# Backward attention: each mask product directly behind its score pair, the dP pair behind both

## Chip, cores, metric

One core of one Trainium2 chip runs the whole kernel. The metric is the time of one execution on the device in microseconds (us). The kernel before takes 2784.18 us (median of 2 executions, 2774.3 to 2794.06). Executions of a kernel on one core are called slow when they are over 1.5% above the fastest of the same kernel, and fast otherwise.

## The reference, cut to what matters

Four residual layers, linear attention (A) and sliding-window attention (B) in turn, forward and then all gradients. The change touches only the backward pass of the two B layers:

```python
scores = einsum("bhqd,bhkd->bhqk", q, k) * (Dh ** -0.5)        # S = 2048, H = 32, Dh = 20, W = 256
mask   = (idx[:, None] - idx[None, :] >= 0) & (idx[:, None] - idx[None, :] < W)
p      = softmax(where(mask, scores, -1e9))
o      = einsum("bhqk,bhkd->bhqd", p, v)
# backward, per block of 128 queries: e = exp(scores + mask), dP = dO v^T, ds = e * dP,
# dv from e, dk and dq from ds
```

## The kernel before

A *unit* is one block of 128 queries of one group of four heads; it sees up to three blocks of 128 keys. There are 8 groups x 16 blocks = 128 units per layer. Four heads fit beside each other in the partitions, 32 rows each, so every score product and every dP product is a matmul on one 32-row tile of TensorE's 128 x 128 array. A half unit is two heads. The steps have short names in this text: **S** scores (2 matmuls of up to 384 columns, 32 rows each), **D** dP (the same shape), **M** mask (2 full-array matmuls of 256 columns that add -30000 where the mask forbids), **F** six transposes of ds (full array), **V** value and key products (16 matmuls on 32-column tiles), **Q** dq products (12 of them).

```python
psl = self.pool(st, "atl", 3)
...
ps_sp = self.pool(st, "pss", 3, PSUM)      # 3 slots: scores and dP tiles
ps_o  = self.pool(st, "pso", 2, PSUM)      # 2 slots: F, V and Q accumulators
...
def scores(u, half, ta, tb):               # S with ("QT","KT"), D with ("dOT","VT")
    ps = ps_sp.tile([P, 2, 512], F32, name="sp")
    for j in range(2):
        r0 = HP * (2 * half + j)           # row tile of the head: 0, 32, 64 or 96
        ...
            nc.tensor.matmul(ps[:, j, ...], lhsT=slabs[..][ta][r0:r0 + HP, qs],
                             rhs=slabs[..][tb][r0:r0 + HP, ...],
                             start=(a == k0), stop=(ta == "dOT"), tile_position=(r0, 0), ...)
    return ps

def mask(u, ps):                           # M
    ...
        nc.tensor.matmul(o, lhsT=self.ident, rhs=self.far, start=False, stop=True, ...)

def expo(u, half, ps):   # ScalarE:  e  = exp(c * ps)          [cut]
def dscore(u, half, ps): # VectorE:  ds = ps * e; for half 0 a DMA transposes ds   [cut]
def flip(u):             # F, for half 1; the copy out is VectorE's in even units, ScalarE's in odd ones
...
for s in range(n + LAG):                   # TensorE runs in exactly this order
    ...                                    # loads cut
    if s < n:
        sc = scores(s, 0, "QT", "KT")
    if 0 <= s - 3 < n:
        dscore(s - 3, 1, scores(s - 3, 1, "dOT", "VT"))
    if s < n:
        mask(s, sc)
        expo(s, 0, sc)
    if 0 <= s - 4 < n:
        flip(s - 4)
    if s < n:
        sc = scores(s, 1, "QT", "KT")
    if 0 <= s - 2 < n:
        dscore(s - 2, 0, scores(s - 2, 0, "dOT", "VT"))
    if s < n:
        mask(s, sc)
        expo(s, 1, sc)
    key_products(s)                        # V
    if 0 <= s - LAG < n:
        dq(s - LAG)                        # Q
```

So a unit is S D M F S D M V Q on TensorE, and the S and D that stand side by side use different halves of the rows.

The softmax here doesn't subtract the row's maximum and nothing guards it: scores larger than these inputs give would overflow.

## Time and profile before

| | before |
|---|---|
| time | 2784.18 us (2774.3 to 2794.06) |
| profiled execution | 2776.2 us, mean granted TensorE clock 0.894 |
| the two stages of the change | 985-1390 and 1720-2125 us |

The table of stretches gives the busy time of each engine in a stretch, then the granted TensorE clock (PEclk, a share of full speed), the DMA share and GB/s. The engines stand in the order PE (TensorE's matmuls), PEld (its weight loads), DVE (VectorE), ACT (ScalarE), POOL (GpSimd), each with its number of instructions behind an x. These are the two stages in the kernel before:

```profile
985.00:1390.00 405.00, 338.82 (x5744) 194.50 (x5744) 280.29 (x384) 274.16 (x448) 3.22 (x6) 0.93 0.77 156
1720.00:2125.00 405.00, 343.39 (x5744) 196.29 (x5744) 280.49 (x384) 274.48 (x448) 1.40 (x3) 0.92 0.77 153
```

TensorE 84%, VectorE 69%, ScalarE 68%: none is full. Next, the page's slices of the span, the granted clock in tenths, one digit for every 69 us. Digits 15 to 20 and 25 to 31 are the stages.

```profile
PEclk9789898778886879999889898999997998999999
```

The groups of instructions of the whole span (busy us, mean ns | idle of the engine before them, and what ended most of it):

```profile
L797 DVE TENSOR_TENSOR ds<-sp,e 128x768 bf16<-128x768 f32 (+2 forms) x512 | 464.5, 907 | 225.7 <-PE sp L758 171.8
L786 ACT ACTIVATE e<-sp 128x768 bf16<-128x768 f32 (+2 forms) x512 | 393.3, 771 | 207.6 <-PE sp L771 146.3
L758 PE MATMUL sp<-VT,dOT 32*128 32x384 bf16 (+2 forms) x1152 | 173.9, 309 | 45.4 <-DVE ds L797 42.2
L758 PE MATMUL sp<-KT,QT 32*128 32x384 bf16 (+2 forms) x1152 | 174.4, 317 | 26.7 <-DMA KT<-qkvT_139 9.7
L771 PE MATMUL sp<-far,ident 128*128 128x256 bf16 x896 | 184.8, 290 | 0.0
```

D (third line) waits for VectorE's product ds. One unit of the timeline, TensorE alone, full clock (start us, us, line, tiles, count, idle before):

```profile
1312.65 0.34 PE L758 MATMUL sp<-KT,QT 32*128 32x384 bf16 x2
1312.88 0.34 PE L758 MATMUL sp<-VT,dOT 32*128 32x384 bf16 x2
1313.15 0.39 PE L771 MATMUL sp<-far,ident 128*128 128x256 bf16 x2
1313.38 0.50 PE L808 MATMUL acc<-ident,ds 128*128 128x128 bf16 x6
1313.82 0.33 PE L758 MATMUL sp<-KT,QT 32*128 32x384 bf16 x2
1314.34 0.34 PE L758 MATMUL sp<-VT,dOT 32*128 32x384 bf16 x2 [0.19 <-DVE ds L797]
1314.61 0.39 PE L771 MATMUL sp<-far,ident 128*128 128x256 bf16 x2
1315.13 0.51 PE L830 MATMUL acc<-e,dOsl 128*32 128x256 bf16 x16
1315.46 0.35 PE L851 MATMUL acc<-dsT,ksl 128*32 128x128 bf16 x12
```

The starts are what counts, since the ends of matmuls are modelled. D to D is 1.46 us (1312.88 to 1314.34). That is one turn of a loop: in the built program every dP tile of this stretch has the same slot in PSUM (where the matmuls write), so D waits until VectorE has read the previous dP tile to form ds.

### The profile page before, as it was taken

What the parts mean: (1) busy time and instruction counts of PE and PEld (TensorE: products, weight loads), DVE (VectorE), ACT (ScalarE), POOL (GpSimd) and SP (SyncE); (2) the same over time, 40 slices, a digit from 0 to 9 for tenths busy, and PEclk for the clock granted to TensorE, in tenths of its full rate; (3) what the DMA queues carried; (4) which work ended last, traced back from release to release, by engine and by line L of the source; (5) the groups of instructions that cost most, each with busy time, mean ns of one, the idle gap of its engine ahead of it and who ended that gap; (6) DMA issues with size and microseconds to landing.
All of it is one profiled execution on the core that took longest, in us unless ns stands there. A gap on an engine that the chain in (4) does not pass through costs nothing.

```text
span 2776.2 us, 66240 instructions
## 1 busy us (share of the span) xinstructions
PE 2305.0 (83%) x27132; PEld 1398.2 (50%) x27132; DVE 1393.4 (50%) x2932; ACT 1379.6 (50%) x2467; POOL 556.5 (20%) x835
## 2 busy tenths in 40 slices
PE   6589998569997578888779696888885987899999
PEld 4345555334544334545447474454543665664654
DVE  6444554333431556777658475776774774500000
ACT  4247666326676357777534464777773445500000
POOL 1124444124455400000033231000001331100000
PEclk9789898778886879999889898999997998999999
DMA  6698886388885878788553575787785448596652
GB/s 204 207 180 172 176 172 164 98 185 180 177 166 140 202 199 161 160 167 157 103 172 127 132 197 178 158 158 159 151 149 145 147 150 197 155 240 152 208 181 66
DMA packets 827824, 457.63 MB, mean 165 GB/s; under 512 B 649088, under 2 KB 771968, under 8 KB 825472
## 3 DMA queue, kind: packets, MB, share of 16 engines
q1 hardware_dynamic: 637568, 237.34, 42.1%
q10 hardware_dynamic: 176768, 168.86, 22.0%
q0 software_dynamic: 13184, 47.20, 5.8%
q8 instruction: 212, 3.47, 0.5%
q14 instruction: 92, 0.75, 0.1%
HBM read 173.41 MB, written 148.50 MB: 116 GB/s over the span
## 4 chain that ended last, share of the span: by engine, by line
PE 53%; DVE 11%; DMA 7%; ACT 7%; issue 4%; POOL 2%; SPq 2%; ACTq 2%; DVEq 0%; POOLq 0%
PE wg L1058 12%; PE d L594 9%; DVE ds L797 6%; PE sp L758 5%; PE d L332 4%; PE acc L830 3%; PE sp L771 3%; PE s L370 3%; ACT dsT L813 3%; PE d L150 2%; PE d L229 2%; PE d L551 2%; PE d L244 2%; ACTq L133 2%; PE d L627 1%
## 5 line engine op out<-in xcount | busy, mean ns | idle before, releaser
L797 DVE TENSOR_TENSOR ds<-sp,e 128x768 bf16<-128x768 f32 (+2 forms) x512 | 464.5, 907 | 225.7 <-PE sp L758 171.8
L786 ACT ACTIVATE e<-sp 128x768 bf16<-128x768 f32 (+2 forms) x512 | 393.3, 771 | 207.6 <-PE sp L771 146.3
L372 ACT ACTIVATE e<-s 128x768 bf16<-128x768 f32 (+2 forms) x512 | 374.2, 774 | 150.2 <-PE s L370 105.1
L1058 PE MATMUL wg<-wg_r,wg_l 128*128 128x480 bf16 (+1 forms) x1920 | 349.3, 345 | 10.6 <-DMA wg_r<-in_grad_out_dram 9.5
L1058 PEld LDWEIGHTS <-wg_l 128*128 128x128 bf16 x1920 | 188.5, 98 | 171.2 <-issue 9.8
L375 POOL TENSOR_SCALAR_AFFINE_SELECT e<-e 128x512 bf16<-128x512 bf16 x256 | 162.7, 635 | 418.7 <-ACT e L372 380.5
L758 PE MATMUL sp<-VT,dOT 32*128 32x384 bf16 (+2 forms) x1152 | 173.9, 309 | 45.4 <-DVE ds L797 42.2
L758 PE MATMUL sp<-KT,QT 32*128 32x384 bf16 (+2 forms) x1152 | 174.4, 317 | 26.7 <-DMA KT<-qkvT_139 9.7
L370 PE MATMUL s<-ring 32*128 32x128 bf16 x2880 | 169.5, 237 | 26.0 <-ACT e L372 24.7
L1062 DVE CAST wg_o<-wg 128x480 bf16<-128x480 f32 (+1 forms) x36 | 21.7, 602 | 335.2 <-PE wg L1058 331.2
L771 PE MATMUL sp<-far,ident 128*128 128x256 bf16 x896 | 184.8, 290 | 0.0
L594 PE MATMUL d<-WT_15475,dqkvT 128*128 128x320 bf16 x960 | 145.7, 307 | 45.2 <-DMA dqkvT<-dqkvT_125 22.7
L1064 ACT CAST wg_o<-wg 128x480 bf16<-128x480 f32 (+1 forms) x24 | 12.3, 514 | 338.8 <-PE wg L1058 338.8
L596 ACT ACTIVATE dh_junk<-d 128x320 bf16<-128x320 f32 x128 | 56.2, 439 | 205.3 <-PE d L594 203.6
L370 PEld LDWEIGHTS <-ring 32*128 32x128 bf16 x2880 | 84.7, 98 | 138.4 <-issue 131.0
L378 POOL TENSOR_SCALAR_AFFINE_SELECT e<-e 128x512 bf16<-128x512 bf16 x224 | 143.2, 639 | 0.0
L244 PEld LDWEIGHTS <-ln_hnT 128*128 128x128 bf16 x960 | 95.7, 106 | 92.5 <-DMA ln_hnT<-ln_hn 35.8
L231 DVE TENSOR_TENSOR car<-d,car 128x320 bf16<-128x320 f32 x128 | 62.2, 486 | 156.0 <-PE d L229 155.3
L758 PEld LDWEIGHTS <-dOT 32*128 32x128 bf16 x1152 | 80.9, 91 | 115.2 <-issue 104.2
L391 PEld LDWEIGHTS <-e 128*128 128x128 bf16 x2880 | 104.2, 98 | 67.5 <-POOL e L378 36.7
L594 PEld LDWEIGHTS <-dqkvT 128*128 128x128 bf16 x960 | 93.3, 100 | 81.2 <-issue 45.7
L808 PE MATMUL acc<-ident,ds 128*128 128x128 bf16 x1440 | 127.9, 225 | 6.0 <-DVE dqkvT_g L837 5.4
(752 smaller groups left out, 4353.1 us busy)
## 6 DMA issues: line engine op xcount, KB each, us to landing
qkvT_135<-ring ACTq DMA_DIRECT2D x16, 768.0 KB
qkvT_139<-ring ACTq DMA_DIRECT2D x16, 768.0 KB
dqkvT_125<-dqkvT_g SPq DMA_DIRECT2D x192, 40.0 KB
dqkvT<-dqkvT_125 POOLq DMA_DIRECT2D x4, 1920.0 KB, 10.2
dqkvT_124<-dqkvT_g SPq DMA_DIRECT2D x192, 40.0 KB
dqkvT<-dqkvT_124 POOLq DMA_DIRECT2D x4, 1920.0 KB, 10.1
wg_r<-dqkv_123 SPq DMA_DIRECT2D x8, 960.0 KB
wg_r<-dqkv_122 SPq DMA_DIRECT2D x8, 960.0 KB
```

What stands on the lines that cost most here:

```text
L244: nc.tensor.matmul(ps, lhsT=hnT[:, k, :], rhs=W[:, k, ci * HD:(ci + 1) * HD], start=(k == 0), stop=(k == self.DT - 1))
L370: nc.tensor.matmul(ps[:, j, i * P:(i + 1) * P], lhsT=ring[r0:r0 + HP, G + g, kt * P:(kt + 1) * P], rhs=ring[r0:r0 + HP, g, qs], start=True ...
L372: nc.scalar.activation(ev[:, 2 * half:2 * half + 2], ps[:, :, 0:nkt * P].rearrange("p h (i q) -> p h i q", q=P), ACT.Exp, scale=self.c_att)
L375: nc.gpsimd.affine_select(out=ev[:, :, nkt - 1, :], in_=ev[:, :, nkt - 1, :], compare_op=ALU.is_ge, fill=0.0, base=0, pattern=[[0, 4], [1, ...
L378: nc.gpsimd.affine_select(out=ev[:, :, 0, :], in_=ev[:, :, 0, :], compare_op=ALU.is_ge, fill=0.0, base=-1, pattern=[[0, 4], [-1, P]], chan ...
L594: nc.tensor.matmul(ps, lhsT=dT[k], rhs=WT[:, k, cs], start=(k == 0), stop=(k == self.QTT - 1))
L758: nc.tensor.matmul(ps[:, j, (a - k0) * P:(z - k0) * P], lhsT=slabs[g, b // HT][ta][r0:r0 + HP, qs], rhs=slabs[g, h][tb][r0:r0 + HP, (a - h ...
L771: nc.tensor.matmul(o, lhsT=self.ident, rhs=self.far, start=False, stop=True, skip_group_check=True)
L786: nc.scalar.activation(ev[:, 2 * half:2 * half + 2], ps[:, :, 0:nkt * P].rearrange("p h (i k) -> p h i k", k=P), ACT.Exp, scale=c_att)
L797: nc.vector.tensor_tensor(out=dv[:, hs], in0=ps[:, :, 0:nkt * P].rearrange("p h (i k) -> p h i k", k=P), in1=ev[:, hs], op=ALU.mult)
L808: nc.tensor.transpose(tp[:, i * P:(i + 1) * P], ds_of[u][:, (nb + i) * P:(nb + i + 1) * P], self.ident)
L1058: nc.tensor.matmul(ps, lhsT=lhs[i][:, tt, m * P:(m + 1) * P], rhs=rhs[i][:, tt, :], start=(i == 0 and tt == 0), stop=(i == len(parts) - 1 ...
```

## The change

The intent is to bring the mask product, and with it exp on ScalarE, forward by one D, and to give each wait more work to hide behind. The instructions stay the same; only their order on TensorE changes (and, as a consequence, which PSUM slot each tile gets).

```diff
                 if s < n:
                     sc = scores(s, 0, "QT", "KT")
+                    mask(s, sc)
+                    expo(s, 0, sc)
                 if 0 <= s - 3 < n:
                     dscore(s - 3, 1, scores(s - 3, 1, "dOT", "VT"))
-                if s < n:
-                    mask(s, sc)
-                    expo(s, 0, sc)
                 if 0 <= s - 4 < n:
                     flip(s - 4)
                 if s < n:
                     sc = scores(s, 1, "QT", "KT")
+                    mask(s, sc)
+                    expo(s, 1, sc)
                 if 0 <= s - 2 < n:
                     dscore(s - 2, 0, scores(s - 2, 0, "dOT", "VT"))
-                if s < n:
-                    mask(s, sc)
-                    expo(s, 1, sc)
                 key_products(s)
```

A unit is now S M D F S M D V Q.

## The prediction

The 0.27, 0.325 and 0.23 us are differences of starts in the trace of the kernel before, and its 480-column matmuls, which start every 0.203 us at full clock, give the 0.16 us for 384 columns. The sum is the 2776 us of the profiled execution (full units stay at 2.91 us) with +10 and +20, about 2805.

> **What bounds it now.** The change touches only the two backward-attention stages, some 800 of 2776 us. The table of stretches shows there, per 100 us, VectorE 73, ScalarE 71 and TensorE 87 us busy: none is full. The timeline of one unit (128 queries, 4 heads) shows why: score pair S, dP pair D, mask pair M, transposes F, then S, D, M, value/key products V, dq products Q; 2.72 and 3.10 us in turn, 2.91 on average. Each D starts within 0.05 us of the end of the previous dP product on VectorE: D to D is 1.45 us. In the built program, for most of the stage all dP tiles sit in one of the three PSUM slots, the scores alternate in the other two, and each D waits on VectorE. Differences of matmul starts: unblocked, D starts 0.006 us behind S (rows 0-63 and 64-127 of the array run together); the mean gap is 0.28 us and the sum 74 us a stage, nearly all this wait.
>
> **What the change does.** Work stays; two things move.
> 1. The slots: the built program now rotates all three. D waits for the exp of the previous scores, S for the dP product two halves back. By durations of the trace (exp starts 0.43 us after M and lasts 0.81 us) neither wait should bind often. The 1.45 us loop goes: gain up to about 72 us a stage.
> 2. The matmul order: S and D no longer stand side by side. M uses the whole array, S and D 32-row tiles. [...] D to M 0.27 us where 384 columns stream in 0.16, M to a 32-row pair 0.325 where M to the full-array F is 0.23. Half a unit thus costs S-M 0.27, M-D 0.325, D-next 0.27 = 0.865 us instead of 0.006+0.27+0.23 = 0.51: about 0.35 us more, times 256 halves, about 85 us a stage (estimate).
>
> **On the critical path.** Adding waits by hand, a full unit after the change takes about 2.8 and 3.0 us in turn, 2.91 on average: as before, but bound by TensorE's own sequence, with V and Q still waiting for the shared accumulator slots. The few units without V gain about 0.2 us; those with two V sets and the narrow first blocks lose 0.2-0.3: about +10 us in all. Where the granted clock is half (about 100 us of these stages), TensorE already binds and D hardly waits, so there only the cost remains: 3.2 us a unit becomes about 4.2, some +20 us.
>
> **Prediction.** 2805 us, 8 in 10 between 2765 and 2850. Faster by over 2%: 0.05; within 2%: 0.80; slower by over 2%: 0.15.
>
> **What would show it.** In the waits, "PE sp waits for DVE ds" (42.8 us, 203 times) nearly vanishes; S-to-M becomes about 0.27 us and M-to-D about 0.33; ScalarE's wait for the mask product (146 us) stays or falls; the stages keep their lengths within 5%; other stages unchanged.
>
> **What would make it wrong.** If mask and dP overlap better than the gaps of before suggest, the freed loop gives up to 70 us back. If V and Q wait longer for their accumulator slots, since F and V now come later against the exp and copy queues, or if TensorE's clock is granted less, 60 us or more are lost.

## The result, and the profile after

The changed kernel takes **3151.79 us** (median of 2 executions, 3147.88 and 3155.7). The ratio to the kernel before is 1.132, with a 95% interval from 1.1137 to 1.1503. (Ratios are the mean time of one kernel's fast executions over that of the other's in the same rounds, so not quite the ratio of the medians that are quoted.) It is 13% slower, where 2805 us, within 2%, was predicted.

| | before | after |
|---|---|---|
| profiled execution | 2776.2 us | 3154.0 us |
| mean granted clock | 0.894 | 0.737 |
| first score matmul of stage 1, from the start | 990.5 us | 997.3 us |
| from there to the first score matmul of stage 2 | 734.4 us | 919.0 us |
| from there to the end | 1051.3 us | 1237.7 us |
| from the start of the last unit of stage 1 to the first score matmul of stage 2 | 359.9 us | 359.5 us |

The span grew by 377.8 us: 6.8 before the first stage, 184.6 and 186.4 in the two parts that hold a stage each. What lies between the stages did not change (last line). So nearly all of it is in the two stages. The stretches of the two stages in the changed kernel, and then its slices (79 us each, so digits 13 to 20 and 25 to 32 are the stages):

```profile
985.00:1590.00 605.00, 568.29 (x5760) 247.64 (x5760) 285.20 (x390) 292.01 (x450) 9.64 (x16) 0.50 0.47 108
1905.00:2515.00 610.00, 568.61 (x5752) 247.85 (x5752) 285.07 (x389) 291.05 (x449) 13.59 (x20) 0.50 0.48 109
```

```profile
PEclk9788987788757555555589895555555598999999
```

The same VectorE and ScalarE work (285 and 292 us a stage against 280 and 274) now takes 600 us, at half clock from end to end: the clock records hold one piece of 0.5 of 583 us in the first stage and one of 597 us in the second. In the kernel before, the longest such piece near the stages is 37 us.

```profile
L797 DVE TENSOR_TENSOR ds<-sp,e 128x768 bf16<-128x768 f32 (+2 forms) x512 | 464.8, 908 | 599.9 <-PE sp L758 499.9
L786 ACT ACTIVATE e<-sp 128x768 bf16<-128x768 f32 (+2 forms) x512 | 394.1, 771 | 473.4 <-PE sp L771 385.0
L771 PE MATMUL sp<-far,ident 128*128 128x256 bf16 x896 | 272.3, 408 | 0.0
L758 PE MATMUL sp<-KT,QT 32*128 32x384 bf16 (+2 forms) x1152 | 246.7, 447 | 25.5 <-DMA KT<-qkvT 19.1
L758 PE MATMUL sp<-VT,dOT 32*128 32x384 bf16 (+2 forms) x1152 | 246.3, 446 | 0.5 <-DVE ds L797 0.5
```

The last line shows that D's wait for VectorE did vanish (45.4 to 0.5 us of idle). Now VectorE and ScalarE wait for TensorE instead. A part of one unit of the timeline after:

```profile
1158.95 0.50 PE L758 MATMUL sp<-KT,QT 32*128 32x384 bf16 x2
1159.38 0.61 PE L771 MATMUL sp<-far,ident 128*128 128x256 bf16 x2
1159.92 0.50 PE L758 MATMUL sp<-VT,dOT 32*128 32x384 bf16 x2
1160.36 0.51 PE L851 MATMUL acc<-dsT,ksl 128*32 128x128 bf16 x12
1160.80 0.50 PE L758 MATMUL sp<-KT,QT 32*128 32x384 bf16 x2
1161.23 0.61 PE L771 MATMUL sp<-far,ident 128*128 128x256 bf16 x2
1161.77 0.50 PE L758 MATMUL sp<-VT,dOT 32*128 32x384 bf16 x2
1162.20 0.82 PE L808 MATMUL acc<-ident,ds 128*128 128x128 bf16 x6
```

S to M is 0.43 us, M to D 0.54, D to the next 0.43. There is no idle mark on any line: TensorE waits for nobody, and still the clock is half. The full unit with V and Q takes 4.65 us: 45 of the 110 units that start between 1050 and 1550 us take just this; the others, some with narrow blocks, without V or with two V, take 3.79 to 5.33.

### The profile page after: what moved, and what is told of

Read it like the earlier page. It is cut to its first block, busy times and chain, and to the rows that moved or that the text cites. A ratio compares the mean times of both kernels' runs of the same rounds, so it can differ in the third digit from the quotient of the medians.

```text
span 3154.0 us, 66204 instructions
## 1 busy us (share of the span) xinstructions
PE 2760.5 (88%) x27132; PEld 1502.0 (48%) x27132; DVE 1396.9 (44%) x2932; ACT 1411.4 (45%) x2467; POOL 556.6 (18%) x835
## 4 chain that ended last, share of the span: by engine, by line
PE 72%; DVE 5%; DMA 5%; issue 3%; ACT 3%; POOL 2%; SPq 1%; ACTq 1%; POOLq 0%; DVEq 0%
PE sp L758 13%; PE wg L1056 11%; PE sp L771 8%; PE d L594 7%; PE acc L808 6%; PE acc L830 5%; PE d L332 4%; PE s L370 3%; PE acc L851 3%; PE d L229 3%; PE d L244 2%; PE d L150 2%; PE d L551 2%; PE d L391 1%; ACT e L372 1%
## 5 line engine op out<-in xcount | busy, mean ns | idle before, releaser
L771 PE MATMUL sp<-far,ident 128*128 128x256 bf16 x896 | 272.3, 408 | 0.0
L758 PE MATMUL sp<-KT,QT 32*128 32x384 bf16 (+2 forms) x1152 | 246.7, 447 | 25.5 <-DMA KT<-qkvT 19.1
L758 PE MATMUL sp<-VT,dOT 32*128 32x384 bf16 (+2 forms) x1152 | 246.3, 446 | 0.5 <-DVE ds L797 0.5
L375 POOL TENSOR_SCALAR_AFFINE_SELECT e<-e 128x512 bf16<-128x512 bf16 x256 | 162.7, 635 | 428.0 <-ACT e L372 425.2
L244 PE MATMUL d<-W,ln_hnT 128*128 128x320 bf16 x960 | 170.4, 336 | 47.6 <-DMA ln_hnT<-ln_hn 34.6
L229 PE MATMUL d<-Wo,oT 128*128 128x320 bf16 x640 | 130.0, 334 | 82.7 <-DMA Wo<-in_A_wo_dram 46.7
L808 PE MATMUL acc<-ident,ds 128*128 128x128 bf16 x1440 | 199.5, 309 | 0.2
L332 PE MATMUL d<-W,ln_hnT 128*128 128x480 bf16 x640 | 194.9, 425 | 0.8 <-DVE car L231 0.8
L594 PE MATMUL d<-WT,dqkvT 128*128 128x320 bf16 x960 | 144.9, 306 | 45.7 <-DMA dqkvT<-dqkvT 45.7
L808 PEld LDWEIGHTS <-ds 128*128 128x128 bf16 x1440 | 132.2, 136 | 78.7 <-issue 77.0
```

What stands on the lines that cost most here:

```text
L229: nc.tensor.matmul(ps[:, 0:self.HD], lhsT=oT[:, k, :], rhs=Wo[:, k, cs], start=(k == 0), stop=(k == self.DT - 1))
L244: nc.tensor.matmul(ps, lhsT=hnT[:, k, :], rhs=W[:, k, ci * HD:(ci + 1) * HD], start=(k == 0), stop=(k == self.DT - 1))
L332: nc.tensor.matmul(ps, lhsT=hnT[:, k, :], rhs=W[:, k, ci * 480:(ci + 1) * 480], start=(k == 0), stop=(k == self.DT - 1))
L594: nc.tensor.matmul(ps, lhsT=dT[k], rhs=WT[:, k, cs], start=(k == 0), stop=(k == self.QTT - 1))
L758: nc.tensor.matmul(ps[:, j, (a - k0) * P:(z - k0) * P], lhsT=slabs[g, b // HT][ta][r0:r0 + HP, qs], rhs=slabs[g, h][tb][r0:r0 + HP, (a - h ...
L808: nc.tensor.transpose(tp[:, i * P:(i + 1) * P], ds_of[u][:, (nb + i) * P:(nb + i + 1) * P], self.ident)
```

## Theories

The waits are gone and the work is the same, so two kinds of theory are left, and a third came up on the way.

- **Theory 1: the clock holds itself down.** In the traces of the two kernels the clock records hold 0.5 and 1.0 only, in pieces that are multiples of 3.413 us on one grid (no border is more than 0.2% of a window off it). So I took windows of that length, and looked for a sum over a window that goes with the clock of the next one. For each window I summed the columns that each matmul streams, times its share of the 128 rows, times its share of the 128 columns of the array: *full-array columns*, at most some 4100 in a window at half clock and 8100 at full (an estimate from the bursts of e1 below, whose 512-column matmuls start every 0.427 and 0.216 us). (Starts moved by 0.1 us, which was chosen because it fits; a matmul across a border split by its streaming time.) Parted at about 3056, a value that was fitted to these traces, the sum of a window tells the clock of the next one. Over all traces, 14 kernels and 11,798 windows, 81 are wrong. Only one of the 81 lies outside 2800 to 3300. A second count from the traces gives 80 of 11,809, about half of them among the 3805 windows at half clock and half among the 8004 at full; so this isn't only a clock that stays as it is. Rival measures do worse at their best parting value: plain columns 2228 wrong, columns times rows 1501, and by the second count columns times the share of the array's columns 1023, the same area without transposes 682. The counts are all that the traces show; why the clock goes with this sum they don't show.
- **Theory 2: the longer sequence itself.** The gaps where 32-row and full-array matmuls follow each other (S to M 0.43 us and M to D 0.54 at half clock) and the lost overlap of S and D (D starts 0.006 us behind S before where nothing holds it, 0.97 us behind it now) cost the time, whatever the clock.
- **Theory 3: the number of mode changes** (changes between 32-row, full-array and 32-column matmuls: eight a unit instead of five) keeps the clock down.

What theory 1 says of the two orders is worked out from the starts. A full unit is 3712 full-array columns: S and D 384 each (4 x 384 x 32/128), M 1024, F 768, V 768, Q 384. In 4.65 us that is 3712 x 3.413 / 4.65 = 2725 a window; the windows of the changed kernel at half clock in stage 1, from its start-up to the last scores, run from 2054 to 2926. In the old order S and D overlap, so that at half clock a unit would take about 4.65 - 0.97 = 3.7 us (an estimate from the same starts: 0.433 + 0.540 + 0.433 for each half become 0.006 + 0.433 + 0.427 or 0.540), some 3400 a window. This is how the first stage begins in both (start of window in us : clock : full-array columns):

```
before  1005:0.5:2512  1008:0.5:2720  1011:0.5:3328  1015:1:3938  1018:1:4460
after   1004:0.5:2569  1007:0.5:2250  1010:0.5:2424  1014:0.5:2536  1017:0.5:2324  1021:0.5:2659 ... for 583 us
```

Both enter the stage at half clock: TensorE has just waited for loads (9.7 us before, 9.6 after, for KT), and the windows that start from 981 to 991 us before, and from 990 to 1000 after, hold 1024 columns at most. The old order reaches 3328 in one window and the next is at full clock; the new one stays at or below 2926 up to its last scores. (Behind the last unit of each stage the clock came up after a window of some 2980, one of the 81 cases that the single value gets wrong: the border is not sharp.) If the clock did come up, the new order could keep it by this count: at full clock, stalls aside, a unit of about 2.9 us is some 4400 a window (an estimate: 3712 x 3.413 / 2.9).

## Experiments

All twelve kernels gave correct results. "Before" in each line is the median of the kernel before on the same chip. Where one execution is named, there was only one. Where a kernel drops to half clock in some executions and not in others, its slower ones carry the label slow; there I list all of them, since the drop is what is studied.

### e1_kick: a burst of array work once per 16 units

```diff
+            def burst(k):
+                acc = ps_o.tile([P, 512], F32, name="acc")
+                for i in range(k):
+                    nc.tensor.matmul(acc, lhsT=self.ident, rhs=self.bmask[:, i % 2, :], start=True, stop=True)
 ...
             for s in range(n + LAG):        # of the changed kernel
+                if s % TT == 8:
+                    burst(24)
```

> The changed kernel plus a burst of 24 full-array matmuls of 512 columns into a spare accumulator, once per 16 units (16 bursts in all, 5 us each at full clock, 10 at half): only more work. Theory 1 (the clock holds itself down: in both traces the clock of a 3.41 us window is full when the window before it saw more than about 3070 full-array columns, and the new order can't reach that at half clock): the clock goes to 1.0 at the first burst of each stage and is 1.0 for most of it; a full unit falls from 4.65 to about 2.9-3.1 us; the kernel gets FASTER by the bursts, 2860 to 2960 us against 3152. Theory 2 [...]: slower by the bursts, 3230 to 3310 us.

Measured: **2865.25 us** (2858.77 to 2872.3, 4 executions), before 2773.87; ratio 1.0342 (1.0309 to 1.0376). Mean clock 0.894. With 384 more matmuls the kernel is 287 us *faster* than the changed kernel (2865.25 against 3151.79, measured in another call). Before its last units the clock did drop three times in stage 1, for 23, 13 and 13 us, and each drop ended inside a burst: the first, from 1212 us, at 1236 us in the burst that starts at 1233.37 us, the others at 1294 and 1403 us in those from 1290.14 and 1399.32 us. Theory 2 is out: the new order at full clock doesn't cost 370 us.

### e2_kick_once and e10_kick_once_again: one burst per stage

The same with `if s == 8:`; e10 is the same kernel again for its scatter.

> The changed kernel plus one such burst per stage, at its ninth unit. Theory 1: the clock rises right after the burst and stays at 1.0 until some sparse stretch (the kernel before has one after 70 to 130 us of full clock, near the units where the value products pile up), then stays at 0.5 to the end of the stage: 2900 to 3100 us, each stage one full-clock stretch and then one long half-clock stretch. Theory 2: no lasting change, 3155 to 3175 us.

> The run with one large burst per stage again, to see its scatter: nothing brings the clock back after a drop in it. 2770 to 2785 us in executions without a drop in the stages; 2850 to 3050 in executions with one. The related kernels (other slots; old order for 16 units) dropped in 3 of 4 executions, so at least one of four should here.

Measured: e2 **2776.22 us** in its single execution (before 2773.87), clock 0.899. In that trace the burst lifts one window to 3698 columns, and then the clock is 1.0 for 358 us in each stage, with no drop; better than I expected, so the range was missed on the fast side. A stretch of the first stage of e2:

```profile
1100.00:1200.00 100.00, 93.91 (x1538) 50.98 (x1536) 72.58 (x102) 73.63 (x122) 0.00 (x0) 1.00 0.88 169
```

VectorE gets through as much per 100 us as in the kernel before (73), with TensorE now the fuller engine. The full unit is 2.80 and 2.91 us in turn, 2.86 on average (all units of stage 1, the narrow ones and those with two V too, 2.92), S to M 0.267, M to D 0.325, D to F 0.268: the sequence that was predicted, once the clock is full.

e10: **2949.56 us** median; its four executions took 3068.31, 2927.79, 2953.1 and 2946.02. So e2's one execution was a lucky one. In the profiled execution of e10 the clock falls after 85 us at full in stage 1 and after 92 us in stage 2, and then stays at half for 426 and 419 us. I had expected at least one execution in four with a drop; by their times and mean clocks (0.777 to 0.834) all four have one, and 3068.31 is above the 3050 that I had put for such executions. So in this trace, as in that of the changed kernel, nothing in the new order brings the clock back before a stage ends.

### e3_same_rows: no overlap, but no more mode changes than before

```diff
                     sc = scores(s, 0, "QT", "KT")           # of the kernel before
-                if 0 <= s - 3 < n:
-                    dscore(s - 3, 1, scores(s - 3, 1, "dOT", "VT"))
+                if 0 <= s - 2 < n:
+                    dscore(s - 2, 0, scores(s - 2, 0, "dOT", "VT"))
 ...
                     sc = scores(s, 1, "QT", "KT")
-                    dscore(s - 2, 0, scores(s - 2, 0, "dOT", "VT"))
+                    dscore(s - 2, 1, scores(s - 2, 1, "dOT", "VT"))
```

In the kernel before, the second piece of a split score product, on the same rows as the first, starts 0.11 us behind it at full clock (median, 256 columns), where a matmul on other rows starts 0.003 to 0.006 us behind.

> The kernel before with the two dP halves exchanged (and one unit earlier for one of them): dP still directly behind the scores, masks behind both, as few changes of tiling mode as before, the dP tiles still in one slot, but scores and dP on the same 32-row groups, so that they can't overlap. Theory 1 (array-area-weighted work per window): at half clock a full unit takes about 4.5 us, some 2800 full-array columns per window, so the clock sticks at 0.5 in both stages and the time is about 3080 to 3150 us. Theory 3 (the number of mode changes holds the clock down): the clock is as in the kernel before and the time within 2% of it.

Measured: **2801.51 us** (one execution; before 2773.87), clock 0.887. My expectation for theory 1 missed: I had put a unit at half clock at 4.5 us. The trace has 4.1 to 4.2 us for units with V at half clock, so some 3020 to 3090 columns a window, right at the parting value. Stage 1 stays at half clock for 47 us (kernel before: 37), until one window holds 3147 and the clock comes up; stage 2 takes 51 us, and a later drop of 20 us heals by itself. The count held here and my estimate of the unit didn't. The run doesn't tell theory 3 from theory 1, as it was meant to. e2 does: with eight mode changes a unit its clock is full for 358 us in each stage.

### e6_quarter_burst: the same burst on a quarter of the array

```diff
-    nc.tensor.matmul(acc, lhsT=self.ident, rhs=self.bmask[:, i % 2, :], start=True, stop=True)
+    nc.tensor.matmul(acc, lhsT=self.ident[0:HP, :], rhs=self.bmask[0:HP, i % 2, :], start=True, stop=True,
+                     tile_position=(0, 0))
```

> The same burst at the same place (24 matmuls of 512 columns, once per stage), but each on one 32-row tile, a quarter of the array: as long and as dense in time, a quarter of the work. If the clock answers to the array-area-weighted columns of a 3.41 us window (threshold about 3060), a window of it holds only some 1024 and the clock stays at 0.5 in both stages: 3150 to 3185 us. If any uninterrupted stretch of busy TensorE raises it, or if the burst helped by shifting the stages in time: 2770 to 2800 us.

Measured: **3171.7 us** (one execution; before 2770.14), clock 0.735. The clock stays at half for 628 and 634 us. The two windows that are full of the burst hold 1024 columns each. A stretch of the first stage of e6, from 76 us behind the end of the burst:

```profile
1100.00:1200.00 100.00, 99.15 (x1016) 43.03 (x1008) 49.74 (x68) 50.41 (x77) 0.00 (x0) 0.50 0.46 104
```

TensorE is busy 99% and has half the clock. In e2 the burst of as many matmuls on the whole array brought its window to 3698 columns, and the clock was 1.0 for 358 us. So in these runs the clock went with how much of the array worked, and not with TensorE being busy without a break. (The bursts differ in rows only. That the share of the array's columns counts too, as in V and Q, rests on the count over all windows.) The run also speaks against the burst having helped by moving the stages in time, since this one lasts at least as long.

### e7_first_half: half of the change

The new order for the first half of the unit only (the first pair of edits of the change), the old one for the second half.

> The change made for the first half of the unit only, the second half as before; nothing added. At half clock a full unit then takes about 4.28 us, on average 2960 full-array columns per window (kernel before 3250, changed 2725). Windows scatter by some 200, so that one passes 3060 within some ten windows and the clock comes up: 2770 to 2810 us, with a first half-clock stretch of each stage longer than in the kernel before. If the loss were proportional to what is moved: about 2960 us.

Measured: **2787.47 us** (one execution; before 2770.14), clock 0.895. Stage 1 begins with 34 us at half clock, up to a window of 3136 columns; one drop of 13 us heals by itself. So half of the change costs 17 us, hardly more than the scatter of the kernel before (2762 to 2778), and the whole 370: the loss isn't proportional to what is moved. (My figure of 3250 a window for the old order in that expectation was low; 3400 is the better estimate.) One detail half missed: the half-clock stretch at the start is not longer than in the kernel before in stage 1 (34 us against 37); in stage 2 it is (47 against 34).

### e8_switch: the old order for 16 units, then the new one

`if s < n and s >= TT` picks the new place of mask and exp, `s < TT` the old; no work is added.

> No work added: the order of the kernel before for the first 16 units of each stage, the changed order for the other 112. If the clock only has to be brought up once: it rises at about the tenth unit as in the kernel before, and the changed order keeps it there (at full clock its windows hold 3070 to 4860 columns): 2760 to 2785 us, clock 0.89 to 0.90. If the changed order itself pulls the clock down: it falls after unit 16 and the time is 3080 to 3130 us.

Measured: **2967.93 us** median; executions 3042.59, 2857.75, 3033.74 and 2902.11 (before 2770.14). Neither expectation holds. In the profiled execution the clock comes up at 1017 us as in the kernel before, and the new order keeps it for a while with 3439 to 4520 columns a window. Then, 78 us later, it falls behind one window of 2688, and it stays down for 460 us. What thinned that window, in the timeline of e8:

```profile
1093.81 0.39 PE L771 MATMUL sp<-far,ident 128*128 128x256 bf16 x2
1095.34 0.23 PE L758 MATMUL sp<-VT,dOT 32*128 32x128 bf16 x2 [1.14 <-ACT e L786]
1095.50 0.83 PE L830 MATMUL acc<-ds,qsl 128*32 128x256 bf16 x16
1096.11 0.54 PE L851 MATMUL acc<-dsT,ksl 128*32 128x128 bf16 x12
```

A single wait of 1.14 us for exp, behind the narrow first blocks of a group. The kernel before has drops as well (from 1096 us for 10 us, from 1874 for 10, from 1977 for 13), and recovers from each in three or four windows. For the new order here one such stall costs the rest of the stage.

### e9_small_kicks: 4 matmuls once per 16 units

`if s % TT == 6: burst(4)` in the changed kernel.

> The changed kernel plus 4 full-array matmuls of 512 columns once per 16 units (64 in all; 0.85 us a time at full clock, 1.7 at half): a sixth of the work of the run with large bursts. At half clock the changed order does 600 to 850 full-array columns per us, so 4 such matmuls in place of 1.7 us of it add some 600-700 to a window of 2300 to 2930: most such windows pass 3060 when the burst lies in one window, about half of them when it is split. So the clock comes up at the first or second burst of a stage and after every drop waits at most one or two bursts: 2790 to 2850 us, between the run with one large burst and the one with sixteen. If the threshold reading is wrong and a burst must fill whole windows: 3150 to 3180 us.

Measured: **2841.24 us** median; executions 2910.96, 2863.45, 2804.23 and 2819.04 (before 2775.51). The median is in the expected range, the two slowest executions are not: in the profiled one, the slowest, more bursts than expected fell short. Two of its windows show the edge. The burst at 1242.20 us brings its window to 3058 columns and the clock stays half; the next, at 1315.86 us, brings its window to 3161 and the clock is full from 1318 us.

### e4_before_rotated and e5_kick_own_slot: the slots alone

The change also moved the PSUM slots. In the built kernel before, 220 of 255 dP tiles of a stage take the slot of the dP tile ahead of them; after the change 38 do, and the rest is mostly a turn of three. e4 gives the old order a strict turn of three, close to the new slots:

```diff
-            ps_sp = self.pool(st, "pss", 3, PSUM)
+            ps_sp = self.pool(st, "pss", 1, PSUM)
+            turn = [0]
 ...
-                ps = ps_sp.tile([P, 2, 512], F32, name="sp")
+                ps = ps_sp.tile([P, 2, 512], F32, name=f"sp{turn[0] % 3}")
+                turn[0] += 1
```

e5 gives the new order, with one burst per stage, slots like the old ones (a pool of two for S, of one for D).

> The kernel before, same order on TensorE, but the three PSUM slots taken strictly in turn, as the changed kernel has them: this is the slot part of the change alone. The dP pair then waits for the exp of the scores of the half before (about 1.29 us from mask to the end of exp, against 0.67 us of TensorE work in between): half a unit about 1.6 us instead of 1.45, the two stages 5 to 10% longer, 2820 to 2870 us; the clock stays near 0.9 since some 3800 columns per window remain. If the slots were the cause of the slowdown: 3100 us or more.

> The changed order with one full-array burst per stage (as in the run with one burst, 2776 us), but with the slots of the kernel before: one PSUM slot for all dP tiles, two for the scores. It measures the slot part of the change once the clock is held equal. The dP pair must again wait for the previous dP product, 1.46 us from dP to dP; TensorE's own sequence from dP to dP is 1.30 us across the transposes and 1.48 across the value and dq products, so a full unit takes about 2.95 us instead of 2.86: 2785 to 2815 us. If the slots don't matter: 2770 to 2785.

Measured: e4 **2834.41 us** (2830.01 to 2852.39, 4 executions), before 2773.87; ratio 1.0252 (1.0203 to 1.03), clock 0.896. As expected: D now waits for exp, which the waits of stage 1 show (us in total, times, longest):

```profile
PE sp L760 <- ACT e L788: 37.3, 108, 1.0
```

So in the old order the old slots are the better ones. The turn of three costs 60 us there with the clock up, so it is not what made the changed kernel slow by 370. e5: 2892.24 us median; executions 2928.19, 2811.56, 2866.37 and 2918.1. The clock of the profiled one drops in stage 2 for 341 us. Its fastest execution, clock 0.898, is in the expected range and 35 us over e2, but those are single executions, and what the slots are worth in the new order stays open.

### e11_pool_mask and e12_pool_mask_filled: can both kernels be beaten?

The runs suggest a kernel: S beside D, and no M on TensorE.

```diff
-            ps_sp = self.pool(st, "pss", 3, PSUM)
+            ps_sp = self.pool(st, "pss", 1, PSUM)     # S
+            ps_d = self.pool(st, "psd", 2, PSUM)      # D
 ...  in expo, after exp of half 1:
+                nc.gpsimd.affine_select(out=ev[:, :, nkt - 1, :], ...)        # e = 0 where the mask forbids
+                if nkt == 3:
+                    nc.gpsimd.affine_select(out=ev[:, :, 0, :], ...)
 ...  in the loop of the kernel before, twice:
-                    mask(s, sc)
```

> An attempt at a faster kernel, from what the runs show: the order of the kernel before (scores and dP side by side), but no mask products on TensorE; GpSimd, idle in these stages, zeroes the masked e instead (two instructions per unit, about 0.64 us each as in the forward stages); the scores get one PSUM slot, the dP tiles two, since without the mask a score tile is free 1.30 us after it starts (0.44 to exp, 0.81 exp) against 1.46 for a dP tile. The bound per half becomes 1.30 instead of 1.46 us: 2.6 to 2.75 us a unit instead of 2.91, 2700 to 2745 us in all, if the clock stays up (at half clock some 2690 columns in 2.7 us are 3400 a window, over the threshold). If GpSimd's writes get in VectorE's way: 2780 us or more.

Measured: **2794.68 us** (2782.23 to 2799.28, 4 executions), before 2775.51; ratio 1.0048 (0.9993 to 1.0104), clock 0.822. TensorE has less to do, and the clock is lower, 0.69 between 1050 and 1370 us where the kernel before has 0.98:

```profile
1050.00:1370.00 320.00, 244.09 (x4264) 152.94 (x4263) 227.86 (x313) 227.10 (x366) 120.40 (x196) 0.69 0.73 146
```

My estimate of 3400 a window at half clock left out the waits: the windows at half clock hold 2112 to 3273. The other outcome that I had named, GpSimd in VectorE's way, is not what happened: VectorE's full product takes 956 ns as in the kernel before (957). The last run fills them with useless work, eight transposes of the identity a unit into columns that nobody reads:

```diff
                 tp = ps_o.tile([P, 1024], BF, name="acc")
+                for i in range(8):
+                    nc.tensor.transpose(tp[:, (6 + i % 2) * P:(7 + i % 2) * P], self.ident, self.ident)
```

> The kernel with the masks on GpSimd (2795 us, clock half for much of the stages, since without the mask products its windows hold 2100 to 2900 columns at half clock) plus 8 useless full-array transposes of 128 columns per unit, written to the unused columns of the accumulator tile ahead of the real transposes: 1024 columns a unit, as much array work as the masks were. At full clock they fill time in which TensorE waits for exp anyway (0.43 us; 1.13 us of TensorE work against 1.30 us from scores to scores). If the clock follows the window's columns: about 3500 a window at half clock, over the threshold, so the clock comes up and stays, a full unit takes 2.6 to 2.8 us, and the kernel takes 2700 to 2750 us, faster than both kernels though it does more. If the columns of transposes don't count for the clock, or the theory is wrong: 2800 to 2860 us.

Measured: **2783.14 us** (2766.51 to 2792.04, 6 executions), before 2778.22; ratio 1.0008 (0.9967 to 1.0049), clock 0.903.

```profile
1050.00:1370.00 320.00, 242.09 (x5360) 182.64 (x5358) 238.25 (x331) 233.39 (x381) 125.33 (x205) 1.00 0.81 153
```

The clock is 1.00 where e11 has 0.69, as theory 1 says if transposes count in the sum. The time is not what I expected. At full clock VectorE does 238 us of work in these 320 us, exactly as much as the kernel before does in the same stretch (238.08), so the pace is the same. The waits of e12 there name what TensorE waits for now: V waits 27.8 us (48 times) for ScalarE's copy of dsT, S 21.3 us for exp. Which of these would have to go was not tried. No version beat the kernel before.

## Why the prediction was wrong

- **Right: the waits.** "'PE sp waits for DVE ds' (42.8 us, 203 times) nearly vanishes": it is 0.5 us, twice.
- **Right: the sequence, at full clock.** "About 2.8 and 3.0 us in turn, 2.91 on average" and "S-to-M becomes about 0.27 us and M-to-D about 0.33": e2, at full clock, has 2.80 and 2.91, 0.267 and 0.325. That trade is about even: e2's one execution takes 2776 us against 2774. The gaps as measured: M to the 32-row D 0.325 us in e2 where M to the full-array F is 0.23 in the kernel before, and D there 0.003 to 0.006 us behind S when nothing holds it.
- **Right: nothing else moves.** From one stage to the next it is 359.9 and 359.5 us, and the first stage starts 6.8 us later.
- **Wrong, and the cause of it all:** "Where the granted clock is half (about 100 us of these stages), TensorE already binds and D hardly waits, so there only the cost remains: 3.2 us a unit becomes about 4.2, some +20 us." The added cost of a unit at half clock was about right (1.0 us predicted; 4.65 us with V against an estimated 3.7 in the old order), its level was not. But I took the *time* at half clock from the old trace, as if it were given from outside. It is 583 + 597 us, not 100. In these traces the clock goes with the array work of the window before: with added work a window of 3698 (e2) and one of 3161 (e9) were followed by full clock, one of 3058 (e9) and those of 1024 (e6) by half. The old order at half clock gets a window of 3328 and the new one none over 2926 up to its last scores, so the half clock at the start of each stage lasted to the stage's end.
- **Wrong as a consequence:** "the stages keep their lengths within 5%" (they grew by about 185 us each), and "ScalarE's wait for the mask product (146 us) stays or falls" (385 us).
- I named the risk "if TensorE's clock is granted less, 60 us or more are lost" and gave it little weight. The trace of before had the numbers to test it: windows of 2512 and 2720 that stayed at half clock, and of 3328 that didn't.

What stays open: what the slots are worth in the new order (e5 dropped in most executions), why e2's one execution had no stall where e10's four did, and the exact weights inside the measure (0.7% of the windows, nearly all close to the parting value, are wrong; among them are those of 2978 and 2975 after which the clock came up at the ends of the two stages).

## What to carry to other kernels

In this case TensorE stayed at half clock under one instruction order, 96 to 99% busy, for 583 and 597 us, until each stage ended; under the other order of the same instructions it left the half clock at the start of a stage in 37 and 34 us, and recovered from each later drop before its last scores in 10 to 13 us. TensorE's busy share didn't show the loss: 94% in the 13% slower kernel's stages (568 of 605 us), 84% in the faster one's. Before a change makes 32-row matmuls stand alone or adds mode changes, work out the full-array columns per 3.4 us window *at half clock* (the measure that fits the traces here), and compare it with the windows of the trace that were and were not followed by full clock. When a small reordering moves the time by far more than its own cost, look at the granted clock first. A measured share of half clock belongs to the old order and must not be carried over to the new one.
